# A Fourier-mixing and squared-ReLU kernel: the Nyquist rows move to GpSimd, each step is squared once in place, and VectorE's queue is reordered

## The chip, the cores and the metric

The kernel runs on one core of one Trainium2 chip. The metric is the device time of the program in microseconds. A core has a matrix engine (TensorE, PE in the profile), VectorE (DVE), ScalarE (ACT), GpSimd (POOL) and SyncE (SP); each works through a queue of its own in order, and they meet at semaphores. SBUF has 128 partitions; matmuls write to PSUM, which is used here as eight banks of 512 float32 columns. DMAs are issued by SP, ACT and POOL.

## The reference

```python
def _attn_ref(x):                      # x: 8 x 3008 x 256, float32
    X = np.fft.fft(x, axis=1)
    X = np.fft.fft(X, axis=2)
    return X.real.astype(np.float32)

def _moe_ref(x, w_in, w_out):          # x: 24064 x 256, w_in: 256 x 2048, w_out: 2048 x 256
    h = np.maximum(x @ w_in, 0.0)
    return (h * h @ w_out).astype(np.float32)
```

The real part of a two-dimensional Fourier transform, over the sequence (3008) and the features (256), goes through a feed-forward layer with a squared ReLU.

## The kernel before

**Symmetry.** The transform of real data is even under a change of sign of both frequencies. The kernel computes for each of 12040 frequencies k (1505 for each of 8 batches) a cosine part `zc` and a sine part `zs`, each with 128 feature frequencies on the partitions. For the row +k the first layer needs P + Q, and for the row -k it needs P - Q, where P comes from `zc` and Q from `zs`. Row 0 of `zs` holds something else: the Nyquist feature frequency, which is even, and so has to keep its sign in the minus half.

**Windows and steps.** The 12040 columns are cut into 25 windows, the first of 240, 512, 512, 240, 512 and 448 columns, the others of 512, the last of 360. A window runs through 8 steps, and a step makes two of the 16 blocks of 128 hidden features. One step has two PSUM banks, `ph`, from a pool of two such pairs. An *ordinary* step is: `pq` (L758: four matmuls, P + Q negated, through the folded weights `gh`), a relu of it, then `turn` (L795: two matmuls with `gh[:, 2]`, which is minus twice the sine weights except for row 0, added onto the same banks, giving P - Q), and a second relu. Both relus are on ScalarE (`relu`, L800), write to one of three `h1` tiles, and VectorE squares each `h1` into `h2` (`power`, L812). The minus half is read in reverse order there.

**Difference steps.** From window 4 on some steps (`diff`, L708: step 5 of windows that fold x, steps 2, 4 and 6 of the others; 51 in all) are made otherwise to relieve ScalarE and PE: `cosines` (L780: two matmuls, P alone), `twice` (L786: VectorE reads P and makes t2 = -2P + n2, the "doubling"), `sines` (L790: two matmuls that add Q to the same banks, and so have to wait for `twice`), ScalarE's relu for the plus half, and a saturating add on VectorE (L807, CUSTOM_DVE) of t2 and the banks for the minus half. n2 is the Nyquist term of each hidden feature. It is made in the same window: at step 0 `spread_nyq` (L768) multiplies `zs` by a selection matrix `sel` so that row 0 stands on all partitions in a PSUM bank, ScalarE copies it to `zn` (L772), and before each difference step `nyq_rows` (L774) has ScalarE scale it by the per-partition weights `g2n`, twice per step (L778).

**What lies between.** Between `pq` or `cosines` and the second group of matmuls, `others(s)` (L819) puts the other work of the step in the queues: the second layer of the window before (`ffn2_steps`, L649: 16 matmuls over 256 columns per step at L665, evicted by ScalarE at L680 and stored by SP), the matmuls of the z units that start in the next window (`z_steps`, L538, evicted by ScalarE, and by VectorE's subtraction `minus`, L578), and the folds. The z matmuls are spread over steps `lo` to `hi` - 1 (L716).

**Folds.** Each batch goes through a first fold in an *x-fold window* (windows 5, 8, 10, 13, 16 and 19 in the steady part): VectorE's `d_even`, `n_cos`, `d_odd`, `n_sin`, `odds` one per step, then `even`, whose result POOL writes to a scratch in DRAM (`scr`, L448), and `back`, in which POOL reads it into `rb` in another order with two direct and two indirect DMAs (L456, L458). `d_odd` lets POOL load the next x. A second fold follows in a *late window* (windows 6, 9, 12, 15, 18 and 21): `fold8` twice and `fold16` twice on VectorE (L472, L483), at steps 2 to 5, and `nyq8` (L485), four two-element copies by POOL. A late window can also have z work: 6, 9 do.

**Order of VectorE's queue around a difference step s** (L832 to L868): the square of the minus half of s - 2, the square of the plus half of s - 1, the fold or z subtraction of s - 1, `twice(s)`, the square of the minus half of s - 1, the fold of s, the saturating add of s, the square of the plus half of s.

Of the kernel before, what the change touches and what calls it, by code (L numbers as in the profile page):

```python
# [29 lines left out]
def kernel(  # L30
# [76 lines left out]
    h1p = ctx.enter_context(tc.tile_pool(name="h1p", bufs=3))  # L107
    h2p = ctx.enter_context(tc.tile_pool(name="h2p", bufs=2))
    wp = ctx.enter_context(tc.tile_pool(name="wp", bufs=2))
    znp = ctx.enter_context(tc.tile_pool(name="znp", bufs=1))  # L110
# [73 lines left out]
    sel = const.tile([P, P], F16, name="sel")  # L184
    nc.gpsimd.memset(sel, 0.0)
    nc.gpsimd.memset(sel[0:1, :], 1.0)
# [183 lines left out]
    def fold_steps(i):  # L370
# [114 lines left out]
        def nyq8():  # L485

            xt, yt = st["xt"], st["yt"]
            for slot in range(2):
                nc.gpsimd.tensor_copy(xt[:, 0, slot, :, 130:131], rev_dim(xt[:, 1, 1 - slot, :, 128:129], 1))  # L489
            nc.gpsimd.tensor_copy(spn[:, 0, :, 0:1], yt[:, 1, 0, :, 128:129])  # L490
            nc.gpsimd.tensor_copy(spn[:, 1, :, 0:1], yt[:, 0, 0, :, 128:129])
# [45 lines left out]

    def z_steps(u, late=False):  # L538
# [15 lines left out]
        def mm(part, h, k, last, o0, o1, lhs, tab):  # L554
            if h == 0 and k == 0:
                st[part] = ps_z.tile([P, 512], F32, name="pz", tag="pz")
# [21 lines left out]
        def minus(part):  # L578
            es, ps = st["es", part], st[part]
# [128 lines left out]
    diff = {w: (5,) if w in fold_at else (2, 4, 6) for w in range(4, NW)}  # L708
    BIG = 3.0e38
    old = None  # L710
    for w in range(NW):
# [4 lines left out]
        lo, hi = 0, NST - 1  # L716
# [23 lines left out]
        elif w in fold_at:  # L740
            fj = fold_jobs(fold_at[w])
            at = [[f] for f in fj[0:5]] + [[], fj[6:7], fj[7:8]]
            post[5] = fj[5:6]
# [4 lines left out]
        if w in late_at:  # L748
            for st in range(4):
                at[st + 2] = at[st + 2] + folds[late_at[w]]["late"][st : st + 1]  # L750
        zj, zl = [], []
        for u in need[w + 1]:
            zu = z_steps(u)
            zj += [(zu, 0, 0), (zu, 1, 0), (zu, 0, 1), (zu, 1, 1)]
# [10 lines left out]
        n2s = {}  # L765
        t2s = {}

        def spread_nyq():  # L768
            pn = ps_z.tile([P, 512], F32, name="pn", tag="pz")
            nc.tensor.matmul(pn[:, 0:wn], sel, zsw[:, 0:wn], start=True, stop=True)  # L770
            zn = n2s["zn"] = znp.tile([P, WN], F16, name="zn", tag="zn")
            nc.scalar.activation(zn[:, 0:wn], pn[:, 0:wn], AF.Copy, bias=0.0, scale=1.0)  # L772

        def nyq_rows(s):  # L774
            n2 = n2s[s] = wp.tile([P, 2, WN], F32, name="n2", tag="w16")
# [91 lines left out]
        if kept:  # L867
            power(*kept)  # L868
# [35 lines left out]
```

## Time and profile before

| | |
|---|---|
| median of 3 runs | 640.88 us (639.75 to 641.47) |
| profiled execution | 640.49 us, span 638.5 us, granted clock 0.994 |
| PE busy | 603.5 us, 4485 matmuls |
| VectorE busy | 472.3 us, 712 instructions |
| ScalarE busy | 476.9 us, 690 instructions |
| GpSimd busy | 75.9 us, 134 instructions |
| ScalarE's n rows, L778 | 102, 67.3 us |
| ScalarE's copy of the spread row, L772 | 21, 12.4 us |
| the spreading matmul, L770 | 21 |
| squares, L814 | 400, 251.9 us |
| doublings, L788; saturating adds, L807 | 51 each, 61.1 and 60.1 us |

The page gives each engine's busy time, and the chain of work that ended last. A group's row gives line, engine, operation, tiles, shapes and count, then busy time and the mean of one in ns, then the idle time of the engine in front of it and what ended that. In the view of the waits a row reads: who waited, for whom, us in total, times, longest. In the timeline a row begins with its start and its length in us from the span's start; a bracket at its end is the idle time before it. A matmul's end in the profile is modelled, so rows of PE overlap: the distance between starts tells what PE spends.

### The profile page before, as it was taken

The numbers are of one execution on the slowest core, as the hardware profiler recorded it, in microseconds if no ns is written. First come the engines' busy times: TensorE is split into PE (matmuls) and PEld (weight loads), VectorE is DVE, ScalarE is ACT, GpSimd is POOL, SyncE is SP. The second block draws the span as 40 slices with busy tenths as digits, with TensorE's granted clock in tenths as the row PEclk, the third lists the DMA queues.
The fourth block names the chain that finished last, engine by engine and source line by source line (L and its number), as shares of the span: only waits on it lengthen the run. The fifth ranks groups of instructions, "written<-read, shape, count | busy, mean of one in ns | idle before, by whom it ended". The sixth has DMA issues, their size and how long they took to land.

```text
span 638.5 us, 11636 instructions
## 1 busy us (share of the span) xinstructions
PE 603.5 (95%) x4485; PEld 431.5 (68%) x4485; DVE 472.3 (74%) x712; ACT 476.9 (75%) x690; POOL 75.9 (12%) x134
## 2 busy tenths in 40 slices
PE   4799998799999999999999999999999999999995
PEld 2456686576677766776667776777767766677784
DVE  7777855896969868768788578877788677787660
ACT  6677767877788777787868787778777877787761
POOL 8202220012000220220003200021000200000000
PEclk9989999999999999999999999999999999999998
DMA  8736331135111731631116411173111311111121
GB/s 152 111 84 126 110 87 43 32 73 158 45 43 35 147 109 34 122 114 54 35 51 120 122 33 49 39 147 96 45 28 56 107 37 38 45 45 49 39 61 55
DMA packets 36543, 47.53 MB, mean 74 GB/s; under 512 B 4232, under 2 KB 30344, under 8 KB 36488
## 3 DMA queue, kind: packets, MB, share of 16 engines
q0 software_dynamic: 9344, 22.14, 17.1%
q1 hardware_dynamic: 26915, 24.44, 12.8%
q8 instruction: 35, 0.57, 0.4%
q10 hardware_dynamic: 228, 0.21, 0.1%
q14 instruction: 21, 0.16, 0.1%
HBM read 33.63 MB, written 27.84 MB: 96 GB/s over the span
## 4 chain that ended last, share of the span: by engine, by line
PE 70%; DVE 15%; ACT 6%; issue 4%; POOL 2%; DMA 1%; ACTq 1%; POOLq 0%; DVEq 0%
PE po L665 38%; PE ph L763 7%; PE ph L762 7%; PE ph L798 7%; DVE h L814 4%; PE ph L793 4%; DVE t L788 4%; ACT h L809 3%; DVE h L807 3%; PE pz L558 3%; PE ph L784 2%; DVE xy L472 1%; ACTq L645 1%; POOL xo L133 1%; PE pn L770 1%
## 5 line engine op out<-in xcount | busy, mean ns | idle before, releaser
L809 ACT ACTIVATE h<-ph 128x1024 f16<-128x1024 f32 (+3 forms) x341 | 315.8, 970 | 73.2 <-PE ph L793 48.4
L665 PE MATMUL po<-wout,h 128*128 128x256 f16 (+1 forms) x3024 | 362.0, 273 | 0.0
L665 PEld LDWEIGHTS <-h 128*128 128x128 f16 (+1 forms) x3024 | 296.8, 98 | 72.0 <-issue 0.6
L814 DVE TENSOR_TENSOR h<-h 128x1024 f16<-128x1024 f16 (+3 forms) x400 | 251.9, 655 | 72.7 <-ACT h L809 67.0
L762 PE MATMUL ph<-zc,gh 128*128 128x512 f16 (+3 forms) x298 | 107.7, 365 | 2.7 <-ACT h L809 1.3
L763 PE MATMUL ph<-zs,gh 128*128 128x512 f16 (+3 forms) x298 | 107.7, 365 | 0.9 <-DVE zs L581 0.7
L807 DVE CUSTOM_DVE_ANT_0 h<-t,ph 128x1024 f16<-128x1024 f32 x47 | 57.4, 1221 | 44.5 <-ACT h L809 43.4
L798 PE MATMUL ph<-zs,gh 128*128 128x512 f16 (+3 forms) x298 | 83.9, 364 | 3.8 <-ACT h L809 2.2
L680 ACT ACTIVATE osb<-po 128x512 f32<-128x512 f32 (+2 forms) x94 | 54.9, 587 | 33.6 <-PE po L665 28.7
L788 DVE SCALAR_TENSOR_TENSOR t<-ph,n 128x1024 f32<-128x1024 f32 (+2 forms) x51 | 61.1, 1199 | 14.0 <-PE ph L784 11.0
L778 ACT ACTIVATE n<-zn,g2n 128x512 f32<-128x512 f16 (+2 forms) x102 | 67.3, 717 | 0.0
L763 PEld LDWEIGHTS <-gh 128*128 128x128 f16 x298 | 29.1, 98 | 34.6 <-issue 3.6
L762 PEld LDWEIGHTS <-gh 128*128 128x128 f16 x298 | 29.1, 98 | 32.4 <-issue 2.0
L793 PE MATMUL ph<-zs,gh 128*128 128x512 f16 (+2 forms) x102 | 29.8, 373 | 10.4 <-DVE t L788 9.8
L798 PEld LDWEIGHTS <-gh 128*128 128x128 f16 x298 | 27.9, 98 | 13.1 <-issue 6.2
L784 PE MATMUL ph<-zc,gh 128*128 128x512 f16 (+2 forms) x102 | 29.9, 375 | 0.0
L772 ACT ACTIVATE zn<-pn 128x512 f16<-128x512 f32 (+2 forms) x21 | 12.4, 589 | 17.7 <-PE pn L770 17.6
L489 POOL COPY xy<-xy 128x2 f16<-128x2 f16 x16 | 2.5, 188 | 164.8 <-DVE xy L472 164.8
L793 PEld LDWEIGHTS <-gh 128*128 128x128 f16 x102 | 9.4, 97 | 16.8 <-issue 14.3
L128 POOL DMA_DIRECT2D xo<-in_x_dram x8 | 6.1, 765 | 119.5 <-DVE fo L423 109.0
L133 POOL DMA_INDIRECT xo<-in_x_dram,idx_r x15 | 18.3, 1218 | 4.5 <-issue 4.3
L784 PEld LDWEIGHTS <-gh 128*128 128x128 f16 x102 | 10.0, 98 | 11.6
(134 smaller groups left out, 344.2 us busy)
## 6 DMA issues: line engine op xcount, KB each, us to landing
out_dram<-osb SPq DMA_DIRECT2D x77, 128.0 KB
xo<-in_x_dram POOLq DMA_DIRECT2D x7, 768.0 KB, 6.7
scr<-ev POOLq DMA_DIRECT2D x8, 390.0 KB, 3.3
rb<-scr POOLq DMA_DIRECT2D x16, 130.0 KB
out_dram<-osb SPq DMA_DIRECT2D x12, 94.0 KB
w<-in_moe_w_in_dram POOLq DMA_DIRECT2D x2, 512.0 KB
wout<-in_moe_w_out_dram POOLq DMA_DIRECT2D x1, 1024.0 KB
out_dram<-osb SPq DMA_DIRECT2D x8, 75.0 KB
```

Of the source, the lines that this page charges most:

```text
L665: nc.tensor.matmul(po[0:m, j * D : (j + 1) * D], h2[:, fc, q : q + m], wout16[:, fc, :], start=(fc == 0), stop=(fc == NFC - 1))
L680: nc.scalar.activation(osb[0:mm].rearrange("p s d -> p (s d)")[:, lo:hi], po[0:mm, lo:hi], AF.Copy, bias=0.0, scale=HS * HS)
L762: nc.tensor.matmul(ph[:, a, 0:wn], gh[:, 0, f0 : f0 + P], zcw[:, 0:wn], start=True, stop=False)
L763: nc.tensor.matmul(ph[:, a, 0:wn], gh[:, 1, f0 : f0 + P], zsw[:, 0:wn], start=False, stop=True)
L778: nc.scalar.activation(n2[:, a, 0:wn], n2s["zn"][:, 0:wn], AF.Copy, bias=0.0, scale=g2n[:, fc : fc + 1])
L784: nc.tensor.matmul(ph[:, a, 0:wn], gh[:, 0, f0 : f0 + P], zcw[:, 0:wn], start=True, stop=True)
L788: nc.vector.scalar_tensor_tensor(out=t2[:, :, 0:wn], in0=phs[s][:, :, 0:wn], scalar=-2.0, in1=n2s[s][:, :, 0:wn], op0=ALU.mult, op1=ALU.add)
L793: nc.tensor.matmul(phs[s][:, a, 0:wn], gh[:, 1, f0 : f0 + P], zsw[:, 0:wn], start=False, stop=True, skip_group_check=True)
L798: nc.tensor.matmul(phs[s][:, a, 0:wn], gh[:, 2, f0 : f0 + P], zsw[:, 0:wn], start=False, stop=True, skip_group_check=True)
L807: nc.vector._custom_dve(TENSOR_ADD_SAT, out=h1[:, :, 0:wn], in0=t2s[s][:, :, 0:wn], in1=phs[s][:, :, 0:wn], s0=BIG, s1=0.0)
L809: nc.scalar.activation(h1[:, :, 0:wn], phs[s][:, :, 0:wn], AF.Relu, bias=0.0, scale=-1.0)
L814: nc.vector.tensor_tensor(h2[:, 2 * s : 2 * s + 2, sg * wn : (sg + 1) * wn], hv, hv, op=ALU.mult)
```

## The change

The Nyquist row of a window is no longer spread by a matmul and scaled by ScalarE in the same window. POOL issues one DMA that reads row 0 of `zs` of the *next* window and writes it to all partitions of `zn` (at step 6), and POOL scales it, twice per difference step: the pair for the first difference step right behind the DMA, the others at step 7, behind `back` in windows that have it. Windows 4 and 5, in front of which z work reaches to the last step, do this in their own step 0. `sel` goes, `wp` (n2) gets three buffers and `znp` two. Window 4 has two difference steps, 4 and 6, instead of three: 50 in all.

`h1` goes: a relu, and the saturating add, write straight into `h2`, the minus half with a reversed output, and `power` squares in place, both halves at once, in the step that follows; only in step 7 are the halves squared apart. VectorE's queue at a difference step s is now: `twice(s)`, then `settle` (the square of all of s - 1 and the z subtractions that `held` kept back during s - 1), the fold of s, the saturating add of s; the square of s comes in step s + 1, behind its `pq`.

The z matmuls end one step earlier (`hi` is 6 instead of 7), sine part before cosine part. In x-fold windows `odds` goes from step 4 to 5 and the Nyquist matmuls `nyq` from 5 to 6. The late folds are at steps 2, 4, 6 and 7 instead of 2 to 5, and the copies of `nyq8` are VectorE's instead of POOL's.

```diff
-    h1p = ctx.enter_context(tc.tile_pool(name="h1p", bufs=3))
-    wp = ctx.enter_context(tc.tile_pool(name="wp", bufs=2))
-    znp = ctx.enter_context(tc.tile_pool(name="znp", bufs=1))
+    wp = ctx.enter_context(tc.tile_pool(name="wp", bufs=3))
+    znp = ctx.enter_context(tc.tile_pool(name="znp", bufs=2))
...
-                nc.gpsimd.tensor_copy(xt[:, 0, slot, :, 130:131], rev_dim(xt[:, 1, 1 - slot, :, 128:129], 1))
-            nc.gpsimd.tensor_copy(spn[:, 0, :, 0:1], yt[:, 1, 0, :, 128:129])
-            nc.gpsimd.tensor_copy(spn[:, 1, :, 0:1], yt[:, 0, 0, :, 128:129])
+                nc.vector.tensor_copy(xt[:, 0, slot, :, 130:131], rev_dim(xt[:, 1, 1 - slot, :, 128:129], 1))
+            nc.vector.tensor_copy(spn[:, 0, :, 0:1], yt[:, 1, 0, :, 128:129])
+            nc.vector.tensor_copy(spn[:, 1, :, 0:1], yt[:, 0, 0, :, 128:129])
...
         def minus(part):
+            if held["on"]:
+                held["jobs"].append(lambda: apart(part))
+            else:
+                apart(part)
...
-    diff = {w: (5,) if w in fold_at else (2, 4, 6) for w in range(4, NW)}
+    diff = {w: (4, 6) if w == 4 else (5,) if w in fold_at else (2, 4, 6) for w in range(4, NW)}
...
+    def spread_nyq(wt):
+        wn1 = wins[wt][1]
+        zn = zns[wt] = znp.tile([P, WN], F16, name="zn", tag="zn")
+        src = zwin(wt)[1][0:1, 0:wn1]
+        nc.gpsimd.dma_start(out=zn[:, 0:wn1], in_=bass.AP(tensor=src.tensor, offset=src.offset, ap=[list(src.ap[0]), [0, P], [1, wn1]]))
+
+    def nyq_rows(wt, steps):
+        wn1 = wins[wt][1]
+        for s in steps:
+            n2 = n2s[wt, s] = wp.tile([P, 2, WN], F32, name="n2", tag="w16")
+            for a in range(2):
+                fc = 2 * s + a
+                nc.gpsimd.tensor_scalar(out=n2[:, a, 0:wn1], in0=zns[wt][:, 0:wn1], scalar1=g2n[:, fc : fc + 1], scalar2=None, op0=ALU.mult)
...
-        lo, hi = 0, NST - 1
+        lo, hi = 0, NST - 2
...
-            at = [[f] for f in fj[0:5]] + [[], fj[6:7], fj[7:8]]
-            post[5] = fj[5:6]
+            at = [[f] for f in fj[0:4]] + [[], fj[4:5], fj[6:7], fj[7:8]]
+            post[6] = fj[5:6]
...
-                at[st + 2] = at[st + 2] + folds[late_at[w]]["late"][st : st + 1]
+                at[(2, 4, 6, 7)[st]] += folds[late_at[w]]["late"][st : st + 1]
...
-            zj += [(zu, 0, 0), (zu, 1, 0), (zu, 0, 1), (zu, 1, 1)]
+            zj += [(zu, 1, 0), (zu, 0, 0), (zu, 1, 1), (zu, 0, 1)]
...
         def relu(s, sg):
-            h1 = h1p.tile([P, 2, 512], F16, name="h1", tag="h1")
+            h = h2[:, 2 * s : 2 * s + 2, sg * wn : (sg + 1) * wn]
+            if sg:
+                h = rev_dim(h, 2)
...
-        def power(s, sg, h1):
-            hv = rev_dim(h1[:, :, 0:wn], 2) if sg else h1[:, :, 0:wn]
-            nc.vector.tensor_tensor(h2[:, 2 * s : 2 * s + 2, sg * wn : (sg + 1) * wn], hv, hv, op=ALU.mult)
+        def power(s, a, b):
+            h = h2[:, 2 * s : 2 * s + 2, a * wn : b * wn]
+            nc.vector.tensor_tensor(h, h, h, op=ALU.mult)
...
+        def nyq(s):
+            if w + 1 in diff and hi < NST - 1:
+                if s == hi:
+                    spread_nyq(w + 1)
+                    nyq_rows(w + 1, diff[w + 1][0:1])
+                elif s == hi + 1:
+                    nyq_rows(w + 1, diff[w + 1][1:])
+            if s == 0 and w in diff and w not in zns:
+                spread_nyq(w)
+                nyq_rows(w, diff[w])
+
+        kept = []
+
+        def settle():
+            for k in kept:
+                power(*k)
+            kept.clear()
+            let_go()
...
+            held["on"] = s0 + ng in diff.get(w, ())
             if s0 in diff.get(w, ()):
                 cosines(s0)
                 twice(s0)
-                if kept:
-                    power(*kept)
+                settle()
                 others(s0)
                 sines(s0)
-                h1a = relu(s0, 0)
-                h1b = relu(s0, 1)
-                power(s0, 0, h1a)
-                kept = (s0, 1, h1b)
-            else:
...
+                relu(s0, 0)
+                relu(s0, 1)
+                kept.append((s0, 0, 2))
+                nyq(s0)
+                continue
+            for s in ss:
+                pq(s)
+            settle()
+            for s in ss:
+                relu(s, 0)
+                if s == NST - 1:
+                    power(s, 0, 1)
+            for s in ss:
+                others(s)
+            nyq(s0)
+            for s in ss:
+                turn(s)
+            for s in ss:
+                relu(s, 1)
+                kept.append((s, int(s == NST - 1), 2))
+        held["on"] = False
+        settle()
```

## The prediction

> **What bounds the kernel now.** I read, in this order, the page (engines, then the chain that ended last), the waits of TensorE (PE), the groups by form, and the timeline of one window.
>
> ```profile
> PE 603.5 (95%) x4485; PEld 431.5 (68%) x4485; DVE 472.3 (74%) x712; ACT 476.9 (75%) x690; POOL 75.9 (12%) x134
> PE 70%; DVE 15%; ACT 6%; issue 4%; POOL 2%; DMA 1%; ACTq 1%; POOLq 0%; DVEq 0%
> ```
> ```profile
> PE ph L793 <- DVE t L788: 9.8, 15, 1.7
> ...
> PE ph L798 <- ACT h L809: 2.2, 5, 1.0
> ```
>
> PE is nearly full. It starts a matmul over 512 columns every 0.215 us and one over 256 every 0.109 us (16 of them fill 1.75 us in the chain of waits); charging all 4485 like this gives 592 us, and 33 us are left in which a start comes late. 14 of those lie in the first 50 us. The largest single group stands before L793, the sines of a "difference step", which wait until VectorE (DVE) has read the cosines (L788, the doubling). The view says 9.8 us; the modelled end of a matmul lies 0.16 us behind its slot, so small gaps vanish: counted start to start over all 51 such steps, PE loses 14.5 us there. How such a gap arises, in step 4 of a late window (one that folds xy):
>
> ```profile
> 461.73 1.22 DVE L807 CUSTOM_DVE_ANT_0 h<-t,ph 128x1024 f16<-128x1024 f32 x1 [0.73 <-ACT h L809]
> ...
> 462.87 1.89 DVE L814 TENSOR_TENSOR h<-h 128x1024 f16<-128x1024 f16 x3
> ...
> 463.51 0.59 PE L784 MATMUL ph<-zc,gh 128*128 128x512 f16 x2
> ...
> 463.94 1.91 PE L665 MATMUL po<-wout,h 128*128 128x256 f16 x16
> ...
> 464.67 0.69 DVE L472 TENSOR_TENSOR xy<-rb 128x1040 f16<-128x1040 f16 x1
> 465.28 1.22 DVE L788 SCALAR_TENSOR_TENSOR t<-ph,n 128x1024 f32<-128x1024 f32 x1
> ...
> 466.55 0.59 PE L793 MATMUL ph<-zs,gh 128*128 128x512 f16 x2 [0.70 <-DVE t L788]
> ```
>
> The cosines end at 464.10, but three squares and a fold stand ahead of the doubling; it starts at 465.28 instead of 464.21. PE's slot was 463.94 + 1.75 = 465.69, the sines start at 466.55: 0.86 us lost. The same 0.86, and 0.59 two steps on, recur in the four late windows without z work; 0.17 to 0.48 us where a z subtraction (L581) is in front.
>
> **The change, part by part.** Rows by form:
>
> ```profile
> L809 ACT ACTIVATE h<-ph 128x1024 f16<-128x1024 f32 x281 | 276.5, 1027 | 60.9 <-PE ph L793 44.2 <-PE ph L798 13.2 <-DVE od L441 1.2
> L814 DVE TENSOR_TENSOR h<-h 128x1024 f16<-128x1024 f16 x336 | 222.1, 687 | 60.5 <-ACT h L809 55.6 <-ACT h L805 2.8 <-issue 0.7
> L778 ACT ACTIVATE n<-zn,g2n 128x512 f32<-128x512 f16 x94 | 62.8, 726 | 0.0
> L419 DVE TENSOR_TENSOR fe<-xo 128x3072 f16<-128x3072 f16 x7 | 12.5, 1786 | 0.2
> L772 ACT ACTIVATE zn<-pn 128x512 f16<-128x512 f32 x19 | 11.3, 597 | 16.1 <-PE pn L770 16.0
> L770 PE MATMUL pn<-zs,sel 128*128 128x512 f16 x19 | 7.2, 379 | 0.0
> ```
>
> *PE work.* The spreading matmul goes: 19 x 0.216 + one of 448 and one of 360 columns (0.19 + 0.15) = 4.4 us, all in PE's queue, which is the bound. Window 4 has two difference steps instead of three; the one made ordinary costs two more matmuls, +0.4. Net -4.0 us on the path.
>
> *ScalarE.* It loses 21 copies (12.4) and 102 row scalings (67.3) and gains one relu (1.0): 477 to about 398 us. PE waits on it little (2.2 us in the line above), so this alone is worth nothing beyond one 0.75 us wait for a free h1 buffer in window 0. Its relu now writes the minus half in reverse. No row has a reversed ScalarE output. Lower bound no cost, as on DVE (L428 with a reversed input, 1560 elements in 0.965 us, is on the same line as L814); upper bound half rate, 1.03 to 1.88 us. I take none.
>
> *Squares.* L814 at 1024 and L419 at 3072 elements give 0.156 us + 0.52 ns per element, so one of 2048 costs 1.22 against two of 0.687. Nine per window instead of 16 (225 instead of 400): -27 us. The four Nyquist copies per batch come from GpSimd (POOL) to DVE: 32 x 0.19 (the 6- and 24-element DVE copies took 0.18 and 0.21) = +6, at step 7, where no doubling follows for at least two steps. One doubling and one saturating add fewer: -2.4. DVE goes from 472 to about 449.
>
> *Order on DVE.* Ahead of the doubling now stands only the saturating add of two steps ago and one square, 1.22 + 1.22. The square of the step just before, held z subtractions and the folds (steps 2, 4, 6, 7) are all queued behind it. In the timeline above: 462.95 + 1.22 = 464.17, so the doubling starts at 464.21, ends 465.43, before 465.69: the 0.86 goes. What is late next? Behind the doubling wait a square 1.22, a fold 0.69, then the saturating add, which needs ScalarE's relu (sines end + 1.0) anyway; DVE's sum over two steps is 4 x 1.22 + 0.69 = 5.6 us, PE's 10 x 0.215 + 32 x 0.109 = 5.65. It fits by a tenth; windows with z matmuls have about half a us more. Of 14.5 us I leave 1.5.
>
> *Moves in the queues.* z now ends a step earlier and sine part first: the same matmuls, 0.1 us more in six steps; at the start of windows 2, 4 and 5 the cosine half is evicted last and PE waits for it first, 0 to 0.3 us each, +0.3 in all. The fold's `odds` and Nyquist matmul go one step later, with two steps to spare. SP's store queue is passed by nothing.
>
> *Rows on POOL.* Added are 21 spreading DMAs (issue about 0.59 each, like scr<-ev) and 100 scalings of 512 elements. POOL's cost per element is bounded below by its iota (377 elements 0.483, 6 elements 0.17: 0.86 ns each, so 0.63 us) and above by its 128-element scaling of 0.84 beside DVE work (0.19 fixed, 5 ns each, 2.75 us). A second effect shows at the start:
>
> ```profile
> 12.55 1.71 POOL L221 TENSOR_SCALAR evs<-evec 128x2 f32<-128x2 f32 x1
> 14.34 0.92 POOL L224 TENSOR_SCALAR wge<-evec 128x2 f32<-128x2 f32 x1
> ...
> 17.39 0.20 POOL L228 TENSOR_TENSOR wge<-wge,wg 128x2 f32<-128x2 f32 x1
> ```
>
> Two elements took 1.71 us: DVE's f16 fold ran from 12.40 to 14.16 and POOL finished 0.1 later; the next ended 0.1 after the next fold; with DVE idle it took 0.20. So a POOL read is held through a DVE square. The other way round, a DVE operation of 1128 elements (L263) beside POOL's 0.85 us scaling took 1.02 us, against 0.75 by its row of 754 elements in 0.549. I take 0.8 us bare, near the iota, the row of most similar length, and 1.3 beside squares; 6 rows then need 8 us of a 25 us window, and most are started a window early. By the Trainium skill, "SBUF — State Buffer", Who interferes with whom, a DVE instruction with two SBUF inputs contends with GpSimd reads, and whoever issues first blocks the other. The rows agree where POOL waited; the block of DVE that it also implies is a rival below.
>
> Only after an x-fold window is this tight. There POOL first waits for DVE's `ev`: in the window with step 2 at 432.9, scr was issued at 425.4. The spread follows at about 425.9; landing 3.0 (the indirect rb<-scr, 130 KB, on the same queue) to 6.7 us (xo, 768 KB); two rows 2.6: ready at 431.5 to 435.2, and the doubling wants them at 433.6. I take 3.0, the row of equal size and queue, and keep both ends; in that one window scr took 6.0 us behind an x load, so 1 us there. Another 1 us for DVE beside POOL.
>
> The Trainium skill, "SBUF — State Buffer", Door 1, gives one port 27.6 GB/s. Since the spread reads one partition 128 times (131 KB), an estimate by that page is 4.7 us plus the fixed part, toward the late end. No trace here shows such a read, and the sum does not use it.
>
> **Sum.** Profiled execution: 640.5 (span 638.5 and 2.0 around it; 0.4 below the median 640.9). 640.5 - 4.0 - 13.0 - 0.75 + 0.3 + 1.0 + 1.0 = **625.0 us**.
>
> **Rivals.**
> - *Late rows (slower).* With landing 6.7 and 1.9 us per row, the first pair is ready at 425.9 + 6.7 + 3.8 = 436.4, the doubling ends 437.6 and PE, free at 435.3, loses 2.3. POOL then does four fold-back DMAs (3.7) and the next pair: 443.9 against 442.4, another 1.2. Six windows (6, 9, 11, 14, 17, 20) x 3.5 = 21, less the 1 counted: 645. It passes the time before from 2.8 us per window on. For it: the queue order; against: rb's 3.0 us. Without the 1.2, 638.
> - *Contention on DVE.* 0.28 us per POOL scaling (1.02 against 0.75) is 28 us on DVE; in the 18 difference steps of late windows the spare tenth is gone, and 18 x 0.28 = 5 us come back: 630. If each square waited out a whole scaling, 18 x 0.8 = 14 us: 639. The Trainium skill's section above would mean the second. The trace shows DVE's f16 operations undisturbed (1.76 with POOL waiting, 1.75 to 1.79 elsewhere), so this is less likely.
> - *The stall only moves.* The square of 1.22 and the fold now stand ahead of the saturating add, which frees the PSUM pair for the doubling after next. If that chain is as long as before, only the 4.0 is gained: 636.5.
> - *Reversed ScalarE writes at half rate.* An ordinary step would take 1.03 + 1.88 + 0.6 = 3.5 us of ScalarE against 3.15 of PE, over 118 steps: +42, 667.
> - *No effect*: the doubling is released as late as now and the rows cost what the matmul did: 640.
>
> **How the numbers follow.** Chances: forecast (618 to 630) 0.55; contention 0.10 (630 to 639); stall moves 0.10; late rows 0.16 (630 to 648); reversed writes 0.06; no effect 0.03. A difference of 0.3%, 1.9 us, is about what this measurement tells from none, so faster means under 639.0. Faster: 0.55 + 0.10 of contention + 0.08 of the moved stall + 0.03 of late rows = 0.76; same: 0.02 of the moved stall, 0.05 of late rows, 0.02 of no effect = 0.09; slower: 0.08 of late rows + 0.06 + 0.01 = 0.15. Range 618 to 641: it leaves out the reversed writes, the worst of the late rows and a little below. The lower end is 625 with the remaining 1.5, 1 and 1 gone and 3 us of startup stalls besides. The likeliest case's own range is 620 to 630.
>
> **What would show it.** L770, L772 and ScalarE's n rows gone, PE's matmul count 4466, ScalarE near 398, DVE near 449 with 225 squares, the long ones 1.22; the wait of the sines on L788's successor under 2 us. Late rows would show as DVE's doubling waiting for POOL n, at step 2 after each x-fold window; contention as squares above 1.22. The forecast is wrong if POOL's rows take over 1.9 us or the spread lands after 6 us or more.

## The result, and the profile after

| | before | changed |
|---|---|---|
| median, same chip | 640.57 us (639.75 to 641.47) | 661.56 us (660.34 to 662.91) |
| profiled execution | 640.49 us, span 638.5 | 660.34 us, span 658.6 |
| granted clock | 0.994 | 0.984 |
| VectorE, ScalarE, GpSimd busy | 472.3, 476.9, 75.9 us | 467.2, 413.9, 276.8 us |
| squares | 400, 251.9 us | 225, 239.0 us |

The changed kernel is slower: 1.0328 times the time before (95% interval 1.0303 to 1.0353), where 625.0 us was forecast, and it lies outside the range of 618 to 641. The engines and the chain that ended last, on the page of the changed kernel:

```profile
PE 606.0 (92%) x4466; PEld 432.4 (66%) x4466; DVE 467.2 (71%) x567; ACT 413.9 (63%) x568; POOL 276.8 (42%) x221
PE 48%; issue 16%; POOL 16%; DMA 9%; ACT 6%; DVE 5%; POOLq 0%; ACTq 0%; DVEq 0%
```

PE has its 4466 matmuls, as forecast, but is on the chain for only 48% of the span instead of 70%, and GpSimd and DMAs, together 3% before, are on it for 25%. The waits say which (who waited, for whom, us in total, times, longest):

```profile
POOL n L735 <- DMA zn<-zs: 119.6, 18, 8.8
...
DVE t L802 <- POOL n L735: 44.7, 11, 6.6
...
PE ph L807 <- DVE t L802: 24.4, 12, 4.3
...
DVE xy L468 <- DMA rb<-scr,idx_r: 8.8, 2, 4.7
...
PE ph L798 <- DVE h L823: 6.2, 2, 3.3
```

Read from top to bottom this is one chain. GpSimd's scaling (L735) waits for the spread row, the doubling (L802) for the scaling, the sines (L807) for the doubling. The last two rows are a branch of it: a late fold waits for `rb`, and the cosines after next wait for the saturating add (L823) that is queued behind that fold. By form, the rows that the forecast had priced:

```profile
L825 ACT ACTIVATE h<-ph 128x1024 f16<-128x1024 f32 x282 | 277.4, 1024 | 103.0 <-PE ph L807 59.7 <-PE ph L812 37.7 <-PE ph L790 4.0
L829 DVE TENSOR_TENSOR h<-h 128x2048 f16<-128x2048 f16 x147 | 183.7, 1249 | 57.5 <-ACT h L825 55.7
L735 POOL TENSOR_SCALAR n<-zn,g2n 128x512 f32<-128x512 f16 x92 | 170.9, 1867 | 126.4 <-DMA zn<-zs 113.1 <-DVE h L829 6.6 <-DVE xy L468 6.4
```

A relu with reversed output costs what a straight one does (mean of both 1.024 us, 1.027 before), a long square 1.249 (forecast 1.22), but a scaling on GpSimd 1.87 instead of 1.3. And the page's list of DMA issues (the last number is the median from issue to landing):

```profile
scr<-ev POOLq DMA_DIRECT2D x8, 390.0 KB, 3.1
zn<-zs POOLq DMA_DIRECT2D x19, 128.0 KB, 6.6
rb<-scr POOLq DMA_DIRECT2D x16, 130.0 KB, 2.4
```

The spread, 128 KB, lands in 6.6 us; the direct `rb<-scr` of 130 KB in 2.4, and the indirect one, which the spread had been priced by, in 3.0 as before. From the start of the spread's issue to the start of the first scaling, which waited for it every time, it is 7.0 us in the median (5.9 to 9.4); in the six x-fold windows, where it stands behind `scr`, 7.4 to 9.4.

One window in full: x-fold window 16 into window 17. GpSimd's timeline (start and length in us, idle time before in brackets):

```profile
440.90 0.59 POOL L444 DMA_DIRECT2D scr<-ev  x1 [3.18 <-DVE od L437]
441.48 0.59 POOL L727 DMA_DIRECT2D zn<-zs  x1
450.84 3.11 POOL L735 TENSOR_SCALAR n<-zn,g2n 128x512 f32<-128x512 f16 x2 [8.77 <-DMA zn<-zs]
453.92 1.12 POOL L452 DMA_DIRECT2D rb<-scr  x2
455.34 1.91 POOL L454 DMA_INDIRECT rb<-scr,idx_r  x1 [0.30 <-issue]
457.55 0.98 POOL L454 DMA_INDIRECT rb<-scr,idx_r  x1 [0.30 <-issue]
458.57 2.64 POOL L735 TENSOR_SCALAR n<-zn,g2n 128x512 f32<-128x512 f16 x1
```

and PE's at the same place:

```profile
448.27 0.59 PE L798 MATMUL ph<-zc,gh 128*128 128x512 f16 x2
...
455.27 1.01 PE L807 MATMUL ph<-zs,gh 128*128 128x512 f16 x2 [4.33 <-DVE t L802]
456.07 0.63 PE L789 MATMUL ph<-zc,gh 128*128 128x512 f16 x1
456.50 0.63 PE L790 MATMUL ph<-zs,gh 128*128 128x512 f16 x1
456.93 0.64 PE L789 MATMUL ph<-zc,gh 128*128 128x512 f16 x1
457.35 0.63 PE L790 MATMUL ph<-zs,gh 128*128 128x512 f16 x1
```

The cosines of step 2 end at 448.87, where the doubling could begin. The row lands at 450.8, two scalings take 3.11, and the sines start at 455.27, 4.5 us late. Behind the scalings stand the four fold-back DMAs, and behind them the rows of the next step. The rows after the wait show one thing more: matmuls of 512 columns now start 0.43 us apart, and the granted clock from 453.8 to 460.6 is 0.50. At the full clock they go like this (same kernel, window 18):

```profile
487.94 0.38 PE L789 MATMUL ph<-zc,gh 128*128 128x512 f16 x1
488.15 0.38 PE L790 MATMUL ph<-zs,gh 128*128 128x512 f16 x1
488.37 0.38 PE L789 MATMUL ph<-zc,gh 128*128 128x512 f16 x1
488.58 0.38 PE L790 MATMUL ph<-zs,gh 128*128 128x512 f16 x1
```

**Where the time went.** As in the prediction I charge each matmul 0.215 us per 512 columns (0.109 per 256) and count from start to start what comes late. All of it in us:

| | before | changed | difference |
|---|---|---|---|
| until the first matmul | 6.7 | 6.4 | -0.3 |
| matmuls at full pace | 591.6 | 587.6 | -4.0 |
| lost in the first 130 us | 21.9 | 18.7 | -3.2 |
| later: sines late | 10.7 | 25.1 | +14.4 |
| later: cosines late, behind the saturating add | 0 | 6.5 | +6.5 |
| later: small delays, 8.8 of them at half the pace | 0 | 9.3 | +9.3 |
| after the last matmul | 7.6 | 4.8 | -2.8 |
| span | 638.5 | 658.6 | +20.1 |

At half the pace a matmul of 512 columns starts 0.21 us late, one of 256 columns 0.10. The 25.1 of the sines sit in six windows, the ones behind an x-fold window: 2.79 and 0.77 in window 6, 2.14 in 9, 2.96 and 2.42 in 11, 2.67 and 2.43 in 14, 4.50 in 17, 3.63 and 0.75 in 20. The 6.5 of the cosines are in windows 6 (3.0) and 9 (3.5).

### The profile page after: what moved, and what is told of

It reads as the page before. It is cut to its first block, busy times and chain, and to the rows that moved or that the text cites. A ratio compares the mean times of both kernels' runs of the same rounds, so it can differ in the third digit from the quotient of the medians.

```text
span 658.6 us, 11186 instructions
## 1 busy us (share of the span) xinstructions
PE 606.0 (92%) x4466; PEld 432.4 (66%) x4466; DVE 467.2 (71%) x567; ACT 413.9 (63%) x568; POOL 276.8 (42%) x221
## 3 DMA queue, kind: packets, MB, share of 16 engines
q0 software_dynamic: 10352, 24.84, 29.4%
## 4 chain that ended last, share of the span: by engine, by line
PE 48%; issue 16%; POOL 16%; DMA 9%; ACT 6%; DVE 5%; POOLq 0%; ACTq 0%; DVEq 0%
PE po L675 27%; POOL n L735 7%; DMA zn<-zs 5%; PE ph L812 5%; PE ph L789 5%; PE ph L790 5%; ACT h L825 3%; POOL rb L454 2%; PE ph L807 2%; POOL xo L132 2%; PE ph L798 2%; PE pz L562 1%; DMA xo<-in_x_dram,idx_c 1%; DVE h L829 1%; DVE t L802 1%
## 5 line engine op out<-in xcount | busy, mean ns | idle before, releaser
L675 PE MATMUL po<-wout,h 128*128 128x256 f16 (+1 forms) x3024 | 365.8, 274 | 0.0
L829 DVE TENSOR_TENSOR h<-h 128x2048 f16<-128x2048 f16 (+7 forms) x225 | 239.0, 1073 | 75.8 <-ACT h L825 73.4
L735 POOL TENSOR_SCALAR n<-zn,g2n 128x512 f32<-128x512 f16 (+2 forms) x100 | 185.6, 1866 | 138.1 <-DMA zn<-zs 119.6
L790 PE MATMUL ph<-zs,gh 128*128 128x512 f16 (+3 forms) x300 | 109.8, 369 | 0.0
L802 DVE SCALAR_TENSOR_TENSOR t<-ph,n 128x1024 f32<-128x1024 f32 (+2 forms) x50 | 60.1, 1202 | 64.6 <-POOL n L735 44.7
L812 PE MATMUL ph<-zs,gh 128*128 128x512 f16 (+3 forms) x300 | 84.2, 363 | 3.6 <-ACT h L821 1.9
L823 DVE CUSTOM_DVE_ANT_0 h<-t,ph 128x1024 f16<-128x1024 f32 x46 | 56.1, 1219 | 15.5 <-ACT h L825 14.7
L790 PEld LDWEIGHTS <-gh 128*128 128x128 f16 x300 | 29.6, 99 | 38.9 <-issue 9.4
L807 PE MATMUL ph<-zs,gh 128*128 128x512 f16 (+2 forms) x100 | 31.0, 393 | 24.4 <-DVE t L802 24.4
L789 PEld LDWEIGHTS <-gh 128*128 128x128 f16 x300 | 29.6, 99 | 32.2 <-issue 1.9
L812 PEld LDWEIGHTS <-gh 128*128 128x128 f16 x300 | 27.1, 97 | 11.5 <-issue 6.2
L444 POOL DMA_DIRECT2D scr<-ev x8 | 4.7, 588 | 69.3 <-DVE od L437 52.6
L807 PEld LDWEIGHTS <-gh 128*128 128x128 f16 x100 | 9.4, 99 | 28.7 <-issue 27.3
L727 POOL DMA_DIRECT2D zn<-zs x21 | 12.3, 588 | 37.8 <-DVE zs L591 25.0
L454 POOL DMA_INDIRECT rb<-scr,idx_r x16 | 22.7, 1421 | 4.9 <-issue 4.9
L567 ACT ACTIVATE es<-pz 128x376 f32<-128x376 f32 (+1 forms) x32 | 15.3, 483 | 14.2 <-PE pz L562 14.1
```

The source lines that it names most:

```text
L675: nc.tensor.matmul(po[0:m, j * D : (j + 1) * D], h2[:, fc, q : q + m], wout16[:, fc, :], start=(fc == 0), stop=(fc == NFC - 1))
L735: nc.gpsimd.tensor_scalar(out=n2[:, a, 0:wn1], in0=zns[wt][:, 0:wn1], scalar1=g2n[:, fc : fc + 1], scalar2=None, op0=ALU.mult)
L789: nc.tensor.matmul(ph[:, a, 0:wn], gh[:, 0, f0 : f0 + P], zcw[:, 0:wn], start=True, stop=False)
L790: nc.tensor.matmul(ph[:, a, 0:wn], gh[:, 1, f0 : f0 + P], zsw[:, 0:wn], start=False, stop=True)
L802: nc.vector.scalar_tensor_tensor(out=t2[:, :, 0:wn], in0=phs[s][:, :, 0:wn], scalar=-2.0, in1=n2s[w, s][:, :, 0:wn], op0=ALU.mult, op1=ALU ...
L807: nc.tensor.matmul(phs[s][:, a, 0:wn], gh[:, 1, f0 : f0 + P], zsw[:, 0:wn], start=False, stop=True, skip_group_check=True)
```

## The experiments

Two theories stood against each other. *Late rows* (L in the expectations): the whole loss is the spread row's late landing and what queues behind it on GpSimd; the squares and the new order gain what the prediction gave them. *Contention*: GpSimd's 100 scalings slow VectorE's instructions, wherever they stand. The expectations' *rival S* is a third: the squares and the new order cost the time. Edits are against the changed kernel unless another is named; each ratio is against the kernel before on the same chip.

### The row by a matmul, scaled by ScalarE, as before; all else changed

```diff
-        nc.gpsimd.dma_start(out=zn[:, 0:wn1], in_=...)
+        pn = ps_z.tile([P, 512], F32, name="pn", tag="pz")
+        nc.tensor.matmul(pn[:, 0:wn1], sel, zwin(wt)[1][:, 0:wn1], start=True, stop=True)
+        nc.scalar.activation(zn[:, 0:wn1], pn[:, 0:wn1], AF.Copy, bias=0.0, scale=1.0)
...
-                nc.gpsimd.tensor_scalar(out=n2[:, a, 0:wn1], in0=zns[wt][:, 0:wn1], scalar1=g2n[:, fc : fc + 1], scalar2=None, op0=ALU.mult)
+                nc.scalar.activation(n2[:, a, 0:wn1], zns[wt][:, 0:wn1], AF.Copy, bias=0.0, scale=g2n[:, fc : fc + 1])
...
+            if s0 + 1 in diff.get(w, ()):
+                nyq_rows(w, (s0 + 1,))
```

> The changed kernel with its Nyquist rows made as before (spread by a matmul and ScalarE at step 0 of the same window, scaled by ScalarE in front of each difference step); one in-place square per step, the order of VectorE's queue and the Nyquist copies on VectorE stay as changed. Theory L (late rows: all of the loss is that the rows of a window behind an x-fold window reach VectorE too late, with the fold-back DMAs behind them and the slower clock after the long waits): PE works 592 us again, the sines lose under 2 us instead of 26.6, so 625 to 631 us, and VectorE never waits for n. Rival S (the squares and the new order cost the time): 650 us or more, with the waits of the sines still above 10 us.

Measured: 625.45 us (625.39 to 625.63), ratio 0.978 (0.9764 to 0.9797). The matmul stands in step 0 of the same window, the scalings ahead of each difference step. The engines on its page, and then the sines' row in its waits and the squares' row by form:

```profile
PE 599.7 (96%) x4487; PEld 431.3 (69%) x4487; DVE 460.2 (74%) x567; ACT 476.7 (76%) x689; POOL 74.7 (12%) x102
```
```profile
PE ph L811 <- DVE t L806: 1.2, 3, 0.6
```
```profile
L833 DVE TENSOR_TENSOR h<-h 128x2048 f16<-128x2048 f16 x147 | 179.7, 1223 | 65.7 <-ACT h L829 62.8 <-issue 0.9
```

Everything that the changed kernel had lost is gone with the rows, and 14 us are gained on the kernel before, although all 21 spreading matmuls are back in PE's queue. Its matmuls at full pace are 592.1 us and later than 130 us it loses 0.7 instead of 40.9. The same window 6 that had to wait for `rb` in the changed kernel shows what the order does where the row is there. VectorE's timeline in the changed kernel:

```profile
156.14 1.23 DVE L802 SCALAR_TENSOR_TENSOR t<-ph,n 128x1024 f32<-128x1024 f32 x1 [4.89 <-POOL n L735]
157.28 1.22 DVE L829 TENSOR_TENSOR h<-h 128x2048 f16<-128x2048 f16 x1
163.21 1.18 DVE L468 TENSOR_TENSOR xy<-rb 128x1040 f16<-128x1040 f16 x1 [4.71 <-DMA rb<-scr,idx_r]
164.31 1.21 DVE L823 CUSTOM_DVE_ANT_0 h<-t,ph 128x1024 f16<-128x1024 f32 x1
```

GpSimd's there:

```profile
152.99 3.12 POOL L735 TENSOR_SCALAR n<-zn,g2n 128x512 f32<-128x512 f16 x2 [6.82 <-DMA zn<-zs]
156.07 1.13 POOL L452 DMA_DIRECT2D rb<-scr  x2
157.50 1.89 POOL L454 DMA_INDIRECT rb<-scr,idx_r  x1 [0.30 <-issue]
159.70 0.98 POOL L454 DMA_INDIRECT rb<-scr,idx_r  x1 [0.30 <-issue]
```

And VectorE's with the rows given back:

```profile
153.66 1.22 DVE L806 SCALAR_TENSOR_TENSOR t<-ph,n 128x1024 f32<-128x1024 f32 x1 [1.52 <-PE ph L802]
154.80 1.21 DVE L833 TENSOR_TENSOR h<-h 128x2048 f16<-128x2048 f16 x1
156.81 0.70 DVE L471 TENSOR_TENSOR xy<-rb 128x1040 f16<-128x1040 f16 x1 [0.80 <-DMA rb<-scr,idx_r]
157.42 1.21 DVE L827 CUSTOM_DVE_ANT_0 h<-t,ph 128x1024 f16<-128x1024 f32 x1
```

GpSimd stood 6.82 us in front of its scaling, and the fold-back DMAs stood behind it: they went out from 156.07 on (from 150.38 with the rows given back), and the fold ran at 163.21 instead of 156.81. That is the branch of 6.5 us; it shows in windows 6 and 9, the only ones in which the late folds follow directly on the x-fold window.

### Matmul or DMA, ScalarE or GpSimd: the other two corners

The first keeps GpSimd's scalings at their places and spreads by the matmul (in the window before); the second keeps the DMA and lets ScalarE scale.

```diff
-        nc.gpsimd.dma_start(out=zn[:, 0:wn1], in_=...)
+        pn = ps_z.tile([P, 512], F32, name="pn", tag="pz")
+        nc.tensor.matmul(pn[:, 0:wn1], sel, zwin(wt)[1][:, 0:wn1], start=True, stop=True)
+        nc.scalar.activation(zn[:, 0:wn1], pn[:, 0:wn1], AF.Copy, bias=0.0, scale=1.0)
```

> The changed kernel with the row spread by the matmul and ScalarE's copy, but at step 6 of the window before, and scaled by POOL at the places of the change. Against the run with rows by PE and ScalarE this has only POOL's scalings more. If the landing makes the loss: 625 to 630 us, with the first pair ready 3.3 us after scr's issue and the second 4.5 + 3.3 us later, each just in time, and small waits for rb in windows 6 and 9. If POOL's queue makes it, 640 or more.

```diff
-                nc.gpsimd.tensor_scalar(out=n2[:, a, 0:wn1], in0=zns[wt][:, 0:wn1], scalar1=g2n[:, fc : fc + 1], scalar2=None, op0=ALU.mult)
+                nc.scalar.activation(n2[:, a, 0:wn1], zns[wt][:, 0:wn1], AF.Copy, bias=0.0, scale=g2n[:, fc : fc + 1])
...
+            if s0 + 1 in diff.get(w, ()):
+                nyq_rows(w, (s0 + 1,))
```

> The changed kernel with the spreading DMA as changed (POOL, step 6 of the window before), but the scaling by ScalarE right in front of each difference step, as it was before the change. If the loss is POOL's queue (1.57 us or more per scaling, fold-back DMAs and rows in each other's way), it is gone but for the landing: the spread lands about 7 us after its issue, in x-fold windows 0 to 2 us later than ScalarE's turn at step 1 of the next window, so ScalarE waits there up to 3 us in six windows: 621 to 632 us, rb in time again. If the landing alone makes the loss, 640 or more.

Measured: 625.17 us (625.07 to 625.32), ratio 0.9774 (0.9756 to 0.9791), and 634.56 us (632.17 to 635.21), ratio 0.9909 (0.988 to 0.9937). With the two kernels already shown:

| us | ScalarE scales | GpSimd scales |
|---|---|---|
| spread by a matmul | 625.45 | 625.17 |
| spread by a DMA at step 6 | 634.56 | 661.56 |

GpSimd's scalings cost nothing where the row is there in time. Its waits and the scalings by line in that run:

```profile
DVE t L806 <- POOL n L739: 1.5, 1, 1.5
```
```profile
L739 POOL TENSOR_SCALAR n<-zn,g2n 128x512 f32<-128x512 f16 (+2 forms) x100 | 180.0, 1814 | 169.2 <-ACT zn L731 168.8
```

They still take 1.81 us each, VectorE is 3.8 us busier than without them (464.0 against 460.2), and the time is the same. That ends contention as the cause. The second corner is a miss by 2.6 us: ScalarE waits for the row in the six windows behind an x-fold window, up to 4.3 us where up to 3 were expected. The DMA costs 9.1 us in the time with ScalarE's rows, 13.6 if the 4.5 us of matmuls that it takes off PE are added. With GpSimd's rows it costs 36.4. The difference of 27 us arises only where the row is late: there two scalings on GpSimd take 3.1 to 3.7 us instead of 1.33 between landing and doubling, and GpSimd's wait for the landing holds up the fold-back and the next rows, which ScalarE's wait does not. No run shows how the 27 us divide between the two. With the DMA and ScalarE the later losses are 10.6 us in the sines, 0 in the cosines and 2.6 in small delays, 1.7 of them at half the pace.

### Each partition reads its own row

The DMA stays where it is and moves as many bytes, but partition p gets row p of `zs` instead of row 0. So the Nyquist term of the difference steps is left out and replaced by other values; the work and its order are the same.

```diff
-        src = zwin(wt)[1][0:1, 0:wn1]
-        nc.gpsimd.dma_start(out=zn[:, 0:wn1], in_=...)
+        nc.gpsimd.dma_start(out=zn[:, 0:wn1], in_=zwin(wt)[1][:, 0:wn1])
```

> The changed kernel with a spread of the same size and queue in which each partition receives its own row of zs instead of row 0 (the Nyquist term of the minus halves in difference steps is left out of the computation by this; all else is as it was). If one source partition sets the landing, it falls from 6.6 to 2.4 to 3.3 us, the first pair of rows comes 3 us earlier, and by theory L the waits at step 2 behind x-fold windows (2.1 to 4.5 us each) nearly vanish: 638 to 648 us. If the landing is set by the queue or by the number of descriptors, it stays near 6.6 and the time at 661.

Measured: 641.51 us (638.82 to 645.1), ratio 1.0033 (1.0005 to 1.0061). From the issue to the scaling that waited it is now 2.98 us in the median (2.13 to 6.53), against 7.02 (5.88 to 9.36) with the one source partition, and GpSimd's waits for it fall from 119.6 us:

```profile
POOL n L734 <- DMA zn<-zs: 46.9, 16, 5.9
```

GpSimd's DMA queue moves 10352 packets and 24.84 MB in both kernels, so it is not their number or size. The single source partition makes 4.0 us of the landing. The prediction's estimate by the Trainium skill, "SBUF — State Buffer", Door 1, was 4.7 us plus the fixed part; the difference measured here, 4.0 us between the medians and 3.75 between the least values, is near it. But only 20 us of the loss of 36 go with it: in the six x-fold windows, where `scr` stands in front, even this DMA takes 2.8 to 6.5 us, and GpSimd's two scalings of 3.1 us follow. What lengthens the landing in these windows stays open; the x load is not all of it, since window 19 has none and took 3.9 us (8.5 in the changed kernel). In window 6 the fold-back is still late (6.1 us of cosines).

### SyncE issues the DMA, at the same place

```diff
-        nc.gpsimd.dma_start(out=zn[:, 0:wn1], in_=...)
+        nc.sync.dma_start(out=zn[:, 0:wn1], in_=...)
```

> The changed kernel with the spreading DMA issued by SP instead of POOL, at the same place of the program. If the 6.6 us of landing come from reading one partition 128 times, they stay at 5.5 to 7 us; if they come from POOL's descriptors and the shared software queue behind the x load and scr, they fall to about 3. Either way the issue no longer stands behind scr in POOL's queue and starts some 3 us earlier in x-fold windows, while the four fold-back DMAs and the second pair of rows keep their order. Theory L: stalls of the sines 26.6 to 5 to 15 us, time 635 to 650. Rival S: no change, 661.

Measured: 653.24 us (651.54 to 654.22), ratio 1.0207 (1.0185 to 1.0228). From issue to first use it is 7.0 us again (5.2 to 8.3), although no x load stands in front of it in its queue. The profiled span is 6.2 us shorter, and the sines are late by 19.1 instead of 25.1; the issuing queue is not what makes the landing long. The expected 635 to 650 was missed: in window 16, say, the issue was not earlier (442.55 against 441.48), because five output stores in front of it in SyncE's queue were being issued from 431.81 to 442.44.

### The DMA a step earlier

One step is 3.2 us of PE's time, about what the first use is late. First with GpSimd's scalings: issued by SyncE, at step 5 in x-fold windows, and with all rows ahead of the fold-back, except in windows 5 and 8.

```diff
-        nc.gpsimd.dma_start(out=zn[:, 0:wn1], in_=...)
+        nc.sync.dma_start(out=zn[:, 0:wn1], in_=...)
...
+                own = 1 if w in fold_at and w + 1 in late_at else 3
-                if s == hi:
+                if s == (hi - 1 if w in fold_at else hi):
                     spread_nyq(w + 1)
-                    nyq_rows(w + 1, diff[w + 1][0:1])
+                if s == hi:
+                    nyq_rows(w + 1, diff[w + 1][0:own])
                 elif s == hi + 1:
-                    nyq_rows(w + 1, diff[w + 1][1:])
+                    nyq_rows(w + 1, diff[w + 1][own:])
```

> The changed kernel with the spread issued by SP, in x-fold windows at step 5 instead of 6, and with all three pairs of rows ahead of the fold-back DMAs, except in windows 5 and 8, where the second fold comes in the next window and only the first pair stays ahead. Theory L: no wait of VectorE for n, no wait for rb beyond 2 us, sines lose under 3 us: 619 to 627 us. Rival S: 655 or more.

Measured: 650.07 us (649.6 to 650.61), ratio 1.0168 (1.0151 to 1.0185): a miss by over 20 us. SyncE's timeline in window 16 says why:

```profile
427.21 10.56 SPq L655 DMA_DIRECT2D out_dram<-osb  x5
437.88 0.48 SPq L727 DMA_DIRECT2D zn<-zs  x1
```

VectorE had written the last `zs` and `zc` in front of it by 429.01, and the spread was issued at 437.88. Five output stores stood in front of it and took 10.56 us to issue, up to 4.3 us for one, where 0.35 is the usual. What had been gained by the earlier place was lost in that queue, and the sines of windows 11 and 17 started 5.0 and 6.7 us late.

Then with GpSimd issuing and ScalarE's rows, where neither queue is in the way (the edit is that of the corner "DMA, ScalarE", with this):

```diff
-            if w + 1 in diff and hi < NST - 1 and s == hi:
+            if w + 1 in diff and hi < NST - 1 and s == (hi - 1 if w in fold_at else hi):
                 spread_nyq(w + 1)
```

> As the run with DMA spread and ScalarE's scaling, but in x-fold windows the spread is issued at step 5, ahead of scr in POOL's queue. The row then lands at about 444.5 on the time axis of the changed kernel, 4 us ahead of its use, and nothing waits for it: PE has 587.6 us of work as in the changed kernel and 20 us of lost slots as in the run with the rows back: 620 to 623 us.

Measured: 624.77 us (622.9 to 629.01), ratio 0.979 (0.9741 to 0.984), 1.8 above the expected range. The runs lay so far apart that it was measured once more, in five rounds:

> The run with the early DMA spread and ScalarE's scaling once more, beside the hybrid: 622.5 to 625 us in the median. If single executions are again up to 629 while the hybrid's stay within 1 us, the landing behind an x load is what varies.

Measured: 623.5 us (622.93 to 623.8), ratio 0.974 (0.9726 to 0.9754). What the 629 of the first was stays open; it did not come back. The late sines are down from 10.6 to 0.4 us in the first trace and 0.8 in the second. One step earlier is worth 11.1 us, so the row was late by less than a step.

### The place of the folds and of the held subtractions

Against the first experiment (matmul and ScalarE): the late folds go back to steps 2 to 5, and z subtractions are not held back.

```diff
-                at[(2, 4, 6, 7)[st]] += folds[late_at[w]]["late"][st : st + 1]
+                at[(2, 3, 4, 5)[st]] += folds[late_at[w]]["late"][st : st + 1]
...
-            held["on"] = s0 + ng in diff.get(w, ())
```

> The run with the rows back on PE and ScalarE (625.5 us), with the late folds at steps 2 to 5 again and no z subtraction held back; one in-place square per step stays. If the queued-back folds and subtractions carry the other part of the gain, the sines lose 5 to 9 us again (a fold of 0.69 us or a subtraction in front of the doubling): 630 to 635 us. If the single square carries all of it, 625 to 627.

Measured: 632.35 us (632.33 to 632.43), ratio 0.9881 (0.9865 to 0.9897). That is 6.9 us more than with the new places, and the sines lose 7.9 us again after the first 130 (0.4 with them). Of the 10.3 us that the sines won after the first 130 (10.7 to 0.4), 7.5 are the place of the folds and subtractions in VectorE's queue.

### Two squares instead of one

Also against the first experiment: the plus half of an ordinary step is squared in its own step, the minus half in the next.

```diff
-                if s == NST - 1:
-                    power(s, 0, 1)
+                power(s, 0, 1)
...
-                kept.append((s, int(s == NST - 1), 2))
+                kept.append((s, 1, 2))
```

> The run with the rows back on PE and ScalarE (625.5 us), with the two halves of each ordinary step squared apart, the plus half in its own step: this puts one square of 0.69 us back in front of the doubling and gives DVE some 110 instructions more. If the single square is what took the sines' waits away, 3 to 8 us of them come back (0.3 to 0.5 us at the steps of late windows without z work): 629 to 634 us. If the queued-back folds and z subtractions did it, 625 to 627.

Measured: 629.33 us (629.13 to 629.37), ratio 0.9838 (0.9821 to 0.9856). The one square per step is worth 3.9 us: with two, VectorE is busy for 471.4 us, the sines lose 3.8 us after the first 130, most of it as 0.31 at steps 4 and 6 of windows that have no z work.

### The version that takes the best of both

ScalarE scales; the row comes by the DMA, except behind the six x-fold windows, where it comes by the matmul.

```diff
+        if wt - 1 in fold_at:
+            pn = ps_z.tile([P, 512], F32, name="pn", tag="pz")
+            nc.tensor.matmul(pn[:, 0:wn1], sel, zwin(wt)[1][:, 0:wn1], start=True, stop=True)
+            nc.scalar.activation(zn[:, 0:wn1], pn[:, 0:wn1], AF.Copy, bias=0.0, scale=1.0)
+            return
...
-            if w + 1 in diff and hi < NST - 1 and s == hi:
+            if w + 1 in diff and hi < NST - 1 and s == hi and w not in fold_at:
                 spread_nyq(w + 1)
```

> Rows scaled by ScalarE; the row spread by DMA in the window before, but behind the six x-fold windows by the matmul and ScalarE's copy at step 0 of the window itself. Where the DMA had too little time it is gone, elsewhere it has more than a window's half: PE has 587.6 + 1.3 us of work and 20 us of lost slots, no wait for n above 0.5 us: 622 to 624 us, with less spread between executions than the run with the early DMA if that spread comes from landings behind x loads.

Measured: 622.85 us (622.69 to 623.1), ratio 0.9732 (0.9718 to 0.9746), the fastest of all, 17.4 us under the kernel before and 38.7 under the changed one. Its page:

```profile
PE 596.9 (96%) x4472; PEld 430.0 (69%) x4472; DVE 460.0 (74%) x567; ACT 469.7 (76%) x674; POOL 84.6 (14%) x117
...
PE 89%; ACT 6%; POOL 2%; DVE 1%; issue 1%; POOLq 0%; DVEq 0%
```

PE is on the chain for 89% of the span: the matmuls at full pace are 588.9 us, and after the first 130 us 0.8 us are lost at most. The early DMA with ScalarE's rows (623.5) has an interval that overlaps with this one's.

## Why the prediction was wrong

**The PE work** was right: 4466 matmuls, 591.6 to 587.6 us, -4.0.

**ScalarE.** Right that nothing hangs on it: with the matmul in place it makes no difference which engine scales (625.45 and 625.17). Its busy time was mis-sized, 413.9 us where 398 were forecast: the copies and scalings overlap their neighbours, and without them the kernel before has 410.9 us of ScalarE, not 397. Reversed writes cost nothing (1.024 us), so that rival (667) is out.

**Squares and the order on VectorE.** Right in mechanism and size. I gave them 13.0 us, 14.5 of the sines' waits down to 1.5. With the rows given back 1.8 are left over the whole run. Two experiments give the parts: the places of folds and subtractions are worth 6.9 us, the single square 3.9. In the changed kernel too, 37 of the 41 difference steps whose row is there start their doubling 0.11 to 0.13 us after the cosines, the other four 0.53 to 0.55. The rival that the stall only moves (636.5) is out. Only VectorE's busy time was mis-sized: forecast at 449, it is 460 without GpSimd's rows and 467 with them. "1.22 against two of 0.687" took the short squares one by one, but in a row they overlap; the three in the timeline that the prediction shows took 1.89, 0.63 each. So the squares save 18.8 us of VectorE without GpSimd's rows (251.9 to 233.1) and 12.9 with them (239.0), instead of 27. (The two rows that gave 0.52 ns per element, 687 and 1786 ns, give 0.54 and a square of 1.24; 1.22 was measured without GpSimd's rows.)

**Rows on GpSimd: the step that failed.** "I take 3.0", the landing of `rb<-scr`, between ends of 3.0 and 6.7. It was 6.6 by the page and 7.0 to first use, at the far end and beyond it. The rule for choosing had been the row of equal size and queue, but size and queue are not what sets it: the same DMA on the other queue takes 7.0, and the same size and queue from 128 source partitions 3.0. What sets it is the property in which the operation differed from every row of the trace, and the prediction had named it ("reads one partition 128 times"), with its estimate by the Trainium skill, "SBUF — State Buffer", Door 1, and left it out of the sum. The second price was off as well: 1.55 us at the least and 1.87 in the mean for a scaling, against 0.8 and 1.3; the iota was no row of similar work. The mean lies in the range given for it, 0.63 to 2.75. But that alone cost nothing where the row was in time (625.17 us with the matmul).

**The rival that came was *late rows*,** with its sign, its place and its condition (2.8 us per window or more) as written. Its price of 3.5 us per window, 645, was still short. After 130 us the changed kernel loses 40.2 us more than the run with the rows given back, 6.7 per window. Three things are behind that. In windows 6 and 9 the fold-back stood behind GpSimd's wait, 6.5 us: the prediction counted the four DMAs as a delay of the rows, but not the rows as a delay of the DMAs. After long waits PE ran at half its pace for a while, 9.3 us, of which nothing was in the sum. And in the six x-fold windows the first use came 7.4 to 9.4 us after the issue, past the far end of 6.7; the sines alone lost up to 5.4 us per window.

**Contention** did not come as a cost in time: long squares went from 1.223 to 1.249 us in the mean, and the scalings cost nothing where the row was in time. The 39 long squares that started while a scaling ran took 1.31 us, so the worse form of that rival, in which each square waits out a whole scaling, did not show. GpSimd was held up more, with 2.26 us for the 38 scalings that started inside a long square and 1.64 for those that met none.

The sum by its terms, against the forecast of 625.0: the sines +25.1 (26.6 instead of 1.5), the cosines +6.5, the small delays +9.3, the two allowances of 1 us -2.0, the rest of the start -0.5, the end -2.8 and what lies around -0.5. That is 35.1, and the profiled execution is 35.3 above the forecast.

## What to carry to other kernels

Where the operation that a change adds has no like in the trace, price it by the property in which it differs from the nearest rows, not by size and queue, and if the two ends of that price give different signs, let the chances say so. A row that one partition had to give to all the others was cheap here by a matmul (0.2 us of PE and a copy of 0.6) and slow by a DMA (7.0 us); if the DMA is wanted, its issue belongs a whole landing (here 7 to 9.4 us) ahead of its use, in a queue with nothing slow in front. And an in-order engine that waits for a landing holds up everything behind it, so look at what is queued there before giving it the wait: with the scalings and their wait on GpSimd the same DMA cost 27 us more than with both on ScalarE.

## What the runs showed of the hardware that was not expected

- A DMA of 128 KB from one partition to all took 7.0 us from issue to first use, one of the same size from 128 partitions to themselves 3.0 (least values 5.9 and 2.1), and the issuing queue made no difference (7.0 by SyncE).
- GpSimd's scaling of 128x512 by a per-partition scalar, float16 to float32, took 1.55 us at its best and 1.87 in the mean.
- SyncE's output stores, which issue in 0.35 us in the median, took up to 4.3 us each in the window shown and up to 7.0 in the changed kernel, and held up the DMA behind them. Why is not shown.
- After some waits PE started its matmuls of 512 columns 0.43 us apart instead of 0.215; the granted clock over the run was 0.984 in the changed kernel and 0.998 with the rows given back. After the first 130 us of the changed kernel the half clock lasted 3.41 or 6.83 us at a time. Of its ten waits of over 2 us, five (2.4 to 4.5 us) brought it and five (2.1 to 3.0 us) did not. What told them apart: cut after 130 us into stretches of 3.41 us, in step with the changes of the granted clock, this kernel has five in which PE had 2.18 us or more without work (charged as above), all followed by half the clock; the others, with 2.00 us or less, were not. In the other runs the two sides are 2.26 and 2.03 us.
